# Weight differences by adding transfers on GpSimd's queue, with the first weights stored with the opposite sign

## The chip, the cores and the metric

The kernel runs on one core of a Trainium2 chip. The metric is the device time of one execution in microseconds (us). Smaller is better. Engine names are those of the profile: PE is TensorE's matmul, PEld its weight load, DVE is VectorE, ACT is ScalarE, POOL is GpSimd, SP is SyncE, which issues the transfers (DMAs).

## The reference: what is computed

A gated recurrence per batch and head gives y, and y, laid out as 3072 tokens by 384 features, goes through a maxout layer:

```python
mag = np.sqrt(a_re * a_re + a_im * a_im)
scale = np.minimum(mag, 0.999) / (mag + 1e-06)
a_re_n, a_im_n = (a_re * scale, a_im * scale)
for t in range(S):                      # S = 768, state S is 48 x 48, complex
    ...
    S_re, S_im = (new_re + kv, new_im)  # new = a * S, kv = k (outer) v
    y[:, :, t] = np.einsum('bhd,bhde->bhe', q[:, :, t], S_re)

h = np.maximum(np.maximum(x @ w1, x @ w2), x @ w3)   # x: 3072 x 384, w: 384 x 768
return (h @ w_out).astype(np.float32)                # w_out: 768 x 384
```

There are 4 batches and 8 heads of 48. The four weights arrive as 64-bit floats and have to be made 32-bit ones. The other inputs are 32-bit.

## The kernel before

**Tiling.** A step g takes 128 tokens of two batches (C = 2, called x and y), and there are 12 steps. Per step, the gates are turned into sums of logarithms and angles (ACT and DVE), queries and keys are scaled, transposed on PE and multiplied, and the state is carried from step to step. The result y, features by tokens, goes through the maxout layer.

**The maxout layer by differences.** max(w1 x, w2 x, w3 x) is w1 x + max(0, (w2 - w1) x, (w3 - w1) x). So ws[1] and ws[2] hold differences, `larger` (line 824) makes max(0, .) on ACT and the second max on DVE, and the part of w1 goes past the maximum as one 384 by 384 matrix wp = w1 times w_out. `product` (line 424) makes wp on PE: T transposes ws[0] block by block, t copies that to `third`, M multiplies by wo into the tiles wm, and m copies wm to wp on ACT. In step 0, `up_one` (line 811) makes the layer for x and y apart, with matmul groups named U, then index f of the 256 columns, then the weight, then x or y: U22y is block 8 times the tokens of y. From step 1 on, `up` takes both together.

**The weights.** `weight_blocks` (line 373) cuts them into 12 blocks of 128 partitions by 768: 0, 3, 6 are w1, 1, 4, 7 are w2, 2, 5, 8 are w3, and 9 to 11 are w_out. The name of a step is W, a letter, and the block. WL loads the 64-bit words with SP. Then, with low and high the halves of each word: a takes the absolute value of high (ACT), b clamps it (DVE), c shifts it left by 3 bits (DVE), d turns low into 2 + low / 2^51 in the block's final place (ACT), e adds the bits of that to the shifted part as integers (DVE), f joins high's sign to the result and writes the block (DVE). For blocks 1, 2, 4, 5, 7, 8 a last step g subtracts w1's block in place, on DVE (line 422).

**What sets the order.** SCHEDULE (line 21) is a text with every step of the program. `program` (line 964) emits them in that order, and `Bound` (line 191) ties each instruction of an engine behind the one emitted before it on the same engine, so each engine runs its own in the order of the text. An instruction waits for its operands, whoever makes them. What concerns POOL: `constants_early` (line 278) runs ahead of the text; then the text has, of POOL's steps, CL (`constants_late`, line 309), Z3, Z4 and Z2 in this order. CL makes the masks maskd and masko, with KB as scratch, and zeroes the two tiles atm. Z3, Z4 and Z2 zero buffers that `third` has used: vbs[3], us["k"][2], vbs[2]. In the text, Wg2 and Wg4 stand at line 32, CL at line 33, the three Z at line 34, Wg5 at line 36, Wg1 at 37, Wg7 at 41 and Wg8 at 42.

The first reader of CL's results is g0x at line 33, a DVE instruction (COPY_PREDICATED atm<-maskd,A) that `scores` (line 688) emits. Behind it on DVE come, among others, mulai and stt (gates of step 1) and uqy, the queries of y that PE then transposes (tpqy). PE's order there is M0, M1, tpqy, M2, tpky.

The profile gives line 200 for nearly every instruction, since `Bound` issues them; they are told apart by tile and operation.

Of the kernel before, what the change touches and what calls it, by code (L numbers as in the profile page):

```python
# [15 lines left out]
AF = mybir.ActivationFunctionType  # L16
OP = mybir.AluOpType
# [119 lines left out]
def kernel(  # L137
# [18 lines left out]
    DM = H * D  # L156
# [31 lines left out]
    T = {}  # L188
# [18 lines left out]
    pe, dve, act, pool, sp = (Bound(e) for e in (nc.tensor, nc.vector, nc.scalar, nc.gpsimd, nc.sync))  # L207
    mm = pe.matmul

    def banks(nm, n=None):  # L210

        ps = psum.tile([P, 2, 512], FP, tag="ps", name=nm)
        T["ps"] = ps
        return ps if n is None else ps.rearrange("p a n -> p (a n)")[:, 0:n]
# [4 lines left out]
    def activation(func, **kw):  # L219

        need = SETS.get(func, T.get("set"))
        if need != T.get("set"):
            act.preload_act_table_set(need)
            T["set"] = need
        act.activation(func=func, **kw)

    def once(key, make):

        if key not in T:
            T[key] = make()  # L230
        return T[key]
# [137 lines left out]
    wp, wo = wx[:, 0:KD], wx[:, KD:]  # L369
# [3 lines left out]
    def weight_blocks():  # L373

        blocks, n = [], FF // 3
        for f in range(3):
            for w, src in zip(ws, (moe_w1, moe_w2, moe_w3)):
                cols = slice(f * n, (f + 1) * n)
                blocks.append((w[:, :, cols], src.rearrange("(i p) m -> p i m", p=P)[:, :, cols]))
        for f in range(0, KF, 2):  # L380
            blocks.append((wo[:, f:f + 2], moe_w_out.rearrange("(i p) m -> p i m", p=P)[:, f:f + 2]))
        return blocks
# [16 lines left out]
    def weight_step(i, step):  # L399

        dst, src = blocks[i]
        n, m = dst.shape[1:]
        raw = T["raw", i].rearrange("p n (m w) -> p n m w", w=2)
        low, high = raw[:, :, :, 0].bitcast(U32), raw[:, :, :, 1]
        ex = xhx[:, 0:KD] if i in EX else xhx[:, KD + KF:]
        ex = ex.rearrange("p f t -> p (f t)").rearrange("p (n m) -> p n m", n=n).bitcast(I32)
        if step == "a":
            activation(out=ex.bitcast(FP), in_=high.bitcast(FP), func=AF.Abs)
        elif step == "b":
            dve.tensor_scalar(out=ex.bitcast(FP), in0=ex.bitcast(FP), scalar1=2.0 ** -15, scalar2=LAST,  # L410
                              op0=OP.max, op1=OP.min)
        elif step == "c":
            dve.tensor_single_scalar(out=ex, in_=ex, scalar=3, op=OP.logical_shift_left)
        elif step == "d":
            activation(out=dst, in_=low, func=AF.Copy, scale=2.0 ** -51, bias=2.0)
        elif step == "e":
            dve.tensor_tensor(out=ex, in0=ex, in1=dst.bitcast(I32), op=OP.add)
        elif step == "f":
            dve.scalar_tensor_tensor(out=dst.bitcast(I32), in0=high, scalar=-0x80000000, in1=ex,
                                     op0=OP.bitwise_and, op1=OP.bitwise_or)  # L420
        else:
            dve.tensor_tensor(out=dst, in0=dst, in1=blocks[i - i % 3][0], op=OP.subtract)

    def product(name, f):

        third = (vbs[2].rearrange("p c i d -> p (c i d)"), vbs[3].rearrange("p c i d -> p (c i d)"),
                 us["k"][2].rearrange("p h d -> p (h d)"))[f][:, 0:2 * DM]
        if name == "T":
            ps = T["wt", f] = banks("wt", 2 * DM)
            for u in range(2):  # L430
                for d in range(KD):
                    o = u * DM + d * P
                    pe.transpose(out=ps[:, o:o + P], in_=ws[0][:, d, (2 * f + u) * P:(2 * f + u + 1) * P], identity=ident)
        elif name == "t":
            act.copy(out=third, in_=T["wt", f])
        elif name == "M":
            for d in range(KD):
                ps = once(("wm", d // 2), lambda: banks("wm"))[:, d % 2, 0:DM]
                for u in range(2):
                    mm(out=ps, lhsT=third[:, u * DM + d * P:u * DM + (d + 1) * P], rhs=wo[:, 2 * f + u],  # L440
                       start=2 * f + u == 0, stop=2 * f + u == KF - 1)
        elif f < 2:
            n = 2 - f
            act.copy(out=wp[:, 2 * f:2 * f + n], in_=T["wm", f][:, 0:n, 0:DM])

    def flat(t):
        return t.rearrange("p c h d -> p (c h d)")
# [473 lines left out]
    def run(name, g):  # L921
# [12 lines left out]
        elif name[0] in "TtMm" and name[1:].isdigit():  # L934
            product(name[0], int(name[1:]))
        elif name[0] == "W":
            i = int(name[2:])
            weight_load(i) if name[1] == "L" else weight_step(i, name[1])
        elif name[0] in "Uu" and name[1:].isdigit():
            up(g, int(name[1]), int(name[2]), name[0])  # L940
        elif name[0] in "Uu" and name[1:3].isdigit():
            up_one(2 * g + "xy".index(name[3]), int(name[1]), int(name[2]), name[0])
        elif name in SEVEN or name in ("ox", "oy") and g > 0:
            seven(g, name)
        elif name[0] == "J":
            join(name[1])
        elif name[-1] in "01" and gates(g, [int(name[-1])], name[:-1]):
            pass
        elif gates(g, list(range(C)), name):
            pass  # L950
        else:
            c = "xy".index(name[-1])
            x, name = g * C + c, name[:-1]
            if name in ("Lr", "Li"):
                load_a(g, c, *(("ar", a_re) if name == "Lr" else ("ai", a_im)))
            elif name in ("Lk", "Lq"):
                load_kq(g, c, *(("k", k) if name == "Lk" else ("q", q)))
            elif name == "Lv":
                load_v(g, c)
            else:  # L960
                assert angles(g, c, name) or turns(g, c, name) or factors(x, name) or scores(x, name) \
                    or state(x, name) or outputs(x, name) or project(x, name), name
# [6 lines left out]
    blocks = weight_blocks()  # L969
# [38 lines left out]
```

## Time and profile before

| what | us |
|---|---|
| median of 3 runs | 585.9 (585.05 to 587.58) |
| span of the profiled execution | 585.0 |
| busy PE | 537.6 (92%) |
| busy PEld | 454.6 (78%) |
| busy DVE | 506.0 (86%) |
| busy ACT | 439.4 (75%) |
| busy POOL | 15.5 (3%) |

The span runs from the first instruction to the last of the profiled execution; the three timed runs took 585.05 to 587.58 us in all. In a timeline, the first column is the start in us from the span's start, the second the duration (of all the instructions, where several in a row are merged and counted with x), then engine, line, operation, output <- inputs, shape, and in brackets how long the engine was idle just before and what it waited for. A tile's name is without its number: w can be any of ws or the gates' tile w. "SPq" is SP's queue of transfers. PEclk is the clock that TensorE was granted, 1.00 for full speed.

### The profile page before, as it was taken

How to read it: one execution, taken by the hardware profiler on the slowest of the kernel's cores; microseconds unless marked ns; L12 is line 12 of the kernel's file. 1: busy time of each engine (PE TensorE's matmuls, PEld its weight loads, DVE VectorE, ACT ScalarE, POOL GpSimd, SP SyncE). 2: the span in 40 equal slices, each digit the busy share in tenths (PEclk: the TensorE clock that was granted, in tenths of full speed). 3: DMA queues.
4: the chain of work that ended last, by engine and by line, in shares of the span. 5: the costliest groups of instructions: out<-in, count | busy, mean ns of one | idle time of the engine just before them, and what ended most of it. 6: DMA issues, size and time to landing. Idle time of an engine off the chain costs nothing.

```text
span 585.0 us, 22777 instructions
## 1 busy us (share of the span) xinstructions
PE 537.6 (92%) x10118; PEld 454.6 (78%) x10118; DVE 506.0 (86%) x784; ACT 439.4 (75%) x740; POOL 15.5 (3%) x50
## 2 busy tenths in 40 slices
PE   2649979898999999999999999999999999999897
PEld 0336668767888888888898888898887888888886
DVE  5999999979898999999889889989998999877504
ACT  7999999857788778788788987887896797643110
POOL 8100100000000000000000000000000000000000
PEclk9778999989999999999999999999999999999999
DMA  8984134414204214223223233143043031010000
GB/s 269 251 181 109 56 85 76 90 33 80 43 18 107 46 35 93 43 48 80 43 53 76 41 62 75 33 97 60 14 97 70 7 73 37 3 43 2 30 0 27
DMA packets 136544, 39.24 MB, mean 67 GB/s; under 512 B 129152, under 2 KB 132224, under 8 KB 136448
## 3 DMA queue, kind: packets, MB, share of 16 engines
q1 hardware_dynamic: 136448, 37.80, 29.2%
q8 instruction: 79, 1.29, 0.9%
q14 instruction: 17, 0.14, 0.1%
HBM read 33.03 MB, written 4.72 MB: 65 GB/s over the span
## 4 chain that ended last, share of the span: by engine, by line
PE 82%; ACT 11%; issue 3%; DMA 1%; DVE 1%; SPq 1%; DVEq 0%; ACTq 0%
PE up L200 31%; PE op L200 22%; PE y L200 6%; PE A L200 5%; PE tp L200 4%; PE dk L200 4%; PE sums L200 3%; PE cs L200 2%; PE wm L200 2%; ACT xhx L200 2%; PE B L200 1%; PE F L200 1%; ACT w L200 1%; ACT e L200 1%; ACT L200 1%
## 5 line engine op out<-in xcount | busy, mean ns | idle before, releaser
L200 PE MATMUL up<-xhx,w 128*128 128x256 f32 x792 | 176.5, 382 | 0.9 <-ACT xhx L200 0.6
L200 PEld LDWEIGHTS up<-xhx,w 128*128 128x128 f32 x792 | 148.7, 190 | 21.6 <-ACT xhx L200 1.1
L200 DVE TENSOR_TENSOR Q<-Q,f 112x512 f32<-112x512 f32 (+2 forms) x72 | 68.3, 952 | 9.4 <-ACT Q L200 9.4
L200 ACT ACT_TABLE_LOAD x48 | 61.6, 1283 | 1.6 <-PEq L992 0.8
L200 PE MATMUL op<-wo,xhx 128*128 128x192 f32 (+1 forms) x220 | 47.4, 363 | 0.0
L200 DVE TENSOR_TENSOR xhx<-xhx,up 128x768 f32<-128x768 f32 x22 | 20.9, 952 | 26.8 <-PE up L200 26.8
L200 PEld LDWEIGHTS op<-wo,xhx 128*128 128x128 f32 x220 | 37.0, 190 | 6.6 <-issue 0.3
L200 PE MATMUL y<-atm,vb 128*32 128x64 f32 x1152 | 39.0, 221 | 2.1 <-issue 2.1
L200 ACT ACTIVATE f<-F 48x280 f32<-48x280 f32 x96 | 38.4, 400 | 3.5 <-DVE g L200 2.3
L200 DVE TENSOR_TENSOR ot<-ot,op 128x192 f32<-128x192 f32 (+1 forms) x66 | 26.7, 418 | 15.7 <-ACT ot L200 12.0
L200 PE MATMUL y<-QG,g 112*32 112x64 f32 x1408 | 38.4, 219 | 0.0
L200 ACT COPY atm<-B 32x128 f32<-32x128 f32 x96 | 24.6, 256 | 18.2 <-DVE atm L200 12.9
L200 PE MATMUL A<-Q,K 112*32 112x80 f32 x1536 | 33.2, 234 | 5.5 <-issue 5.5
L200 ACT COPY ot<-op 128x192 f32<-128x192 f32 (+1 forms) x13 | 4.5, 344 | 44.2 <-PE op L200 44.2
L200 PEld LDWEIGHTS y<-atm,vb 128*32 128x32 f32 x1152 | 32.4, 109 | 6.4 <-issue 3.4
L200 PEld LDWEIGHTS A<-Q,K 112*32 112x32 f32 x1536 | 28.0, 110 | 10.4 <-issue 9.1
L200 PEld LDWEIGHTS y<-QG,g 112*32 112x32 f32 x1408 | 34.9, 109 | 1.3 <-issue 1.2
L200 PE MATMUL op<-wo,strassen 128*128 128x192 f32 x176 | 33.5, 332 | 0.3 <-issue 0.3
L200 DVE COPY_PREDICATED atm<-masko,A 128x256 f32<-128x256 uint8 x72 | 31.1, 432 | 1.1
L200 ACT COPY Q<-tp 112x1024 f32<-112x1024 f32 x24 | 24.4, 1019 | 8.7 <-PE tp L200 8.7
L200 PEld LDWEIGHTS op<-wo,strassen 128*128 128x128 f32 x176 | 28.6, 190 | 3.0 <-issue 2.1
L200 PE MATMUL op<-w,strassen 128*128 128x192 f32 x176 | 30.7, 327 | 0.0
(145 smaller groups left out, 1144.0 us busy)
## 6 DMA issues: line engine op xcount, KB each, us to landing
ar<-in_a_re_dram SPq DMA_DIRECT2D x24, 192.0 KB
ai<-in_a_im_dram SPq DMA_DIRECT2D x24, 192.0 KB
q<-in_q_dram SPq DMA_DIRECT2D x96, 48.0 KB
vb<-in_v_dram SPq DMA_DIRECT2D x96, 48.0 KB
k<-in_k_dram SPq DMA_DIRECT2D x96, 48.0 KB
out_dram<-ot SPq DMA_DIRECT2D x24, 192.0 KB
w<-in_moe_w_dram SPq DMA_DIRECT2D x3, 768.0 KB
xhx<-in_moe_w_dram SPq DMA_DIRECT2D x3, 768.0 KB
```

Source lines behind the costliest of these rows:

```text
L200: ins = f(*a, **kw)
```

## The change

The w1 blocks (0, 3, 6) are made with the opposite sign: step d gives -(2 + low / 2^51), so the sign bit is set, and step f flips it by high's sign with an exclusive or. The difference w2 - w1 is then a sum, w2 + (-w1), and step g is a transfer from SBUF to SBUF that adds its source to its destination, issued on GpSimd's queue in place of DVE's subtraction. Since wp is made from w1, the copies of wm to wp turn the sign back. SCHEDULE is as it was.

```diff
         elif step == "d":
-            activation(out=dst, in_=low, func=AF.Copy, scale=2.0 ** -51, bias=2.0)
+            sign = -1.0 if i in (0, 3, 6) else 1.0
+            activation(out=dst, in_=low, func=AF.Copy, scale=sign * 2.0 ** -51, bias=sign * 2.0)
         elif step == "e":
             dve.tensor_tensor(out=ex, in0=ex, in1=dst.bitcast(I32), op=OP.add)
         elif step == "f":
             dve.scalar_tensor_tensor(out=dst.bitcast(I32), in0=high, scalar=-0x80000000, in1=ex,
-                                     op0=OP.bitwise_and, op1=OP.bitwise_or)
+                                     op0=OP.bitwise_and, op1=OP.bitwise_xor)
         else:
-            dve.tensor_tensor(out=dst, in0=dst, in1=blocks[i - i % 3][0], op=OP.subtract)
+            pool.dma_start(out=dst, in_=blocks[i - i % 3][0], accum_op=OP.add)
...
             n = 2 - f
-            act.copy(out=wp[:, 2 * f:2 * f + n], in_=T["wm", f][:, 0:n, 0:DM])
+            activation(out=wp[:, 2 * f:2 * f + n], in_=T["wm", f][:, 0:n, 0:DM], func=AF.Copy, scale=-1.0)
```

The source and the destination of one transfer are 128 partitions of three runs of 256 floats, 384 KB.

## The prediction

> **What bounds the kernel now.** I read the page's 40 slices first, then busy times by stretch, then the chain of work that ended last, then the timelines of the engines that the change touches.
>
> ```profile
> PE   2649979898999999999999999999999999999897
> DVE  5999999979898999999889889989998999877504
> ACT  7999999857788778788788987887896797643110
> ```
>
> One digit is 14.6 us. PE is full from slice 7 (102 us) to the end, and the whole chain is 82% PE, so what happens earlier counts by how late it makes PE. The edited steps end before 99 us, where DVE and ACT are both at 9. The stretch from 52 to 101 us (length, then busy PE, PEld, DVE, ACT, POOL, then clock, DMA share, GB/s) says the same: ACT is idle for only 1.7 us of 49, DVE for 2.8.
>
> ```profile
> 52.00:101.00 49.00, 44.24 (x837) 35.19 (x826) 46.21 (x71) 47.26 (x80) 1.64 (x3) 1.00 0.37 87
> ```
>
> The chain there is PE from 48 to 66.6 us, ACT to 87.9, then PE.
>
> ```profile
> 52.93 7.94 PE wm L200 x24
> 60.87 0.59 PE tp L200 x16
> 61.46 4.07 PE wm L200 x12
> ...
> 66.59 0.87 ACT K L200
> ```
>
> **What is removed.** Six subtractions leave DVE (Wg2, Wg4 at 52.05 us, Wg5 73.18, Wg1 77.39, Wg7 91.94, Wg8 97.89). They start 0.87 us apart from the next instruction, so DVE gets back 6 x 0.87 = 5.2 us. I count it at nothing, apart from one term below: after the first two DVE waits anyway (mulw at 54.49 stands until ACT's L, which does not move), and around the other four the chain runs through ACT. If ACT did not cover it, 5.2 us would be the most that could be won.
>
> The edits of sign cost nothing: bitwise_xor takes bitwise_or's place in the same two-input instruction (0.95 us), the activation of step d has other constants, and the two copies of wm to wp (128x384 in 0.48 us, 128x768 in 0.80) become activations, whose rows of these sizes read 0.49 to 0.51 and 0.81 to 0.85. At worst 0.06 us each on ACT.
>
> **What is moved: the constants on POOL.** This is the step that decides. POOL takes its instructions in order:
>
> ```profile
> 8.40 0.41 POOL L200 MEMSET KB<- 128x384 f32 x1
> ...
> 15.53 1.28 POOL L200 MEMSET atm<- 128x512 f32 x2
> 60.99 0.75 POOL L200 MEMSET vb<- 128x768 f32 x1 [44.18 <-PE wm L200]
> 65.59 0.21 POOL L200 MEMSET uk<- 128x128 f32 x1 [3.85 <-PE wm L200]
> 65.73 0.74 POOL L200 MEMSET vb<- 128x768 f32 x1
> ```
>
> The last line is Z2. Its buffer was last read by the first 12 of the 24 wm matmuls, so it was free at about 57 us; it ran at 65.73, behind Z4, which waited. A waiting instruction holds what follows. In SCHEDULE, Wg2 and Wg4 stand ahead of CL (the masks and the zeroed atm). Today CL has nothing ahead of it and runs at 8.40. After the change it stands behind two transfers, whose operands are finished by these:
>
> ```profile
> 50.32 0.95 DVE L200 SCALAR_TENSOR_TENSOR w<-xhx 128x768 int32<-128x768 int32 x1
> 51.19 0.95 DVE L200 SCALAR_TENSOR_TENSOR w<-strassen,xhx 128x768 int32<-128x768 int32 x1
> ...
> 55.83 0.72 DVE L200 COPY_PREDICATED atm<-maskd,A 128x512 f32<-128x512 uint8 x1
> ```
>
> The third line is g0x, the first reader of CL. From CL's start to the end of the first atm memset is 15.53 + 0.64 - 8.40 = 7.8 us. Let D be the time that POOL spends on issuing one transfer. Then CL starts at 51.27 + 2D (not before 52.14 + D), and g0x is late by 51.27 + 2D + 7.8 - 55.83 = 3.2 + 2D.
>
> No POOL transfer is in this trace. The nearest rows are SP's issues: a weight load, also 384 rows, takes 0.37 us at its shortest; the longest took 5.28 us, behind nine others. So D lies between 0.37 and 2.64 (two in a row taking what that one took). SP's short rows are nearest in form, but part 3 calls their queue hardware_dynamic, GpSimd's would not be that, and a transfer that adds reads two operands. I take the geometric middle of 0.37 and 5.28, 1.4 us. **g0x is late by 6.0 us** (4.5 to 8.5).
>
> DVE is in order, so everything behind g0x is as late: mulai and stt, for which ACT's L (59.57) and atan (60.30) wait; and uqy (59.44), for which PE's transposition at 60.80 waits, 0.4 us behind it. ACT and PE have no idle time to take this up. Below I give times in the old frame, with this delay left out.
>
> **PE's clock.** PE now stands idle for about 5.5 us at 60.9. Today's trace has a 1.67 us gap at 115.45, with this behind it (same columns):
>
> ```profile
> 118.00:122.00 4.00, 4.00 (x9) 2.16 (x8) 3.96 (x8) 2.38 (x4) 0.00 (x0) 0.61 0.01 4
> ```
>
> The granted clock fell to 0.61 for 4 us: 4 x 0.39 = **1.6 us** lost. I add it once, on the 12 wm matmuls, which ACT's K waits for. It could be 0: gaps of 1.2 us cost nothing.
>
> **The four later transfers.** Each has an issue D and a landing T on the path that the subtraction's 0.95 us had. T: the first load of 192 KB was used 2.9 us after its issue began, the first of 768 KB 6.3 us after, so 384 KB lies at 4.0 by size, less SP's 0.44 of issuing: T = 3.5 (2.5 to 6.3). D + T = 4.9.
> - Wg1 and Wg5 stand behind Wf5 (ends 72.79): 72.79 + 2.8 + 3.5 = 79.1. U01x starts at 79.61, U12x at 81.67. In time by 0.5.
> - Wg7: Wf7 ends 89.76, lands 94.7. U21y starts at about 93.7, the third of three groups of 12 from 90.84. Late by 1.0.
> - Wg8: Wf8 ends 97.64, here 0.87 earlier as Wg7 no longer stands ahead of it on DVE: 96.77 + 4.9 = 101.7. U22y:
>
> ```profile
> 99.34 1.60 PE L200 MATMUL up<-xT,w 128*128 128x128 f32 x12
> ```
>
> Late by **2.3 us**, Wg7's 1.0 within it (0 to 6). From here PE is full, so it stays. By the Trainium skill (DMA: Bandwidth & Descriptors, "Anatomy of one DMA — SWDGE (gpsimd) path") such a transfer costs about 2.0 us fixed plus its bytes at 436 GB/s, 2.9 us for 384 KB; with that for D + T, Wg8 would be late by 0.3 and the sum 2 us lower. No run here shows one yet.
>
> **Sum.** 6.0 + 1.6 + 2.3 = 9.9 us on a span of 585.0. The profiled execution's span lies 0.9 us under the median, 585.9; I take that as the time around it and predict 585.9 + 9.9 = 595.8.
>
> **Rivals.**
> - *Cheap transfers* (D = 0.37, D + T = 2.9, clock not lost): 4.5 + 0.3 = 4.8, so 590.7. For it: SP's short rows. Against: SP's queue is not GpSimd's. 0.18.
> - *Dear transfers* (D = 2.64, T = 6.3): g0x 8.5, Wg8 96.77 + 8.94 - 99.34 = 6.4, clock 1.6: 16.5, so 602.4; if issuing is slower still, above that. The DMA share is 0.86 from 52 to 56 us, so there is traffic to share with. 0.13.
> - *Faster*: POOL does not stand at a transfer's wait but hands it to a queue, so CL is done by 55.83 as today, and DVE's 5.2 us is what bounds the stretch from 73 to 98. It decides from the point where ACT and PE wait for DVE there rather than DVE for them. At most 585.9 - 5.2 = 580.7. Against: the order Z4, Z2 above, and ACT idle for only 1.7 us. 0.04.
> - *No difference*: CL is in time as in that case and ACT covers DVE, with at most ACT's idle 1.7 us won: 584.2 to 586. 0.07.
>
> **Chances.** Forecast (592 to 600) 0.58, and the rivals as given. The range 589 to 603 takes in the bounds of D and T and leaves out the last two rivals and about half of the dear one. A measurement here tells about 0.5%, 2.9 us, from no change: faster 0.04, same 0.07, slower 0.89.
>
> **What would show it.** In the profile after: POOL's memset of KB at 53 to 55 us instead of 8.40, and the atm memsets at 60 to 63; DVE's idle time before COPY_PREDICATED atm<-maskd put down to POOL, some 5 to 7 us; PE's transposition tp<-uq 6 us later, and the granted clock lower behind that gap; PE waiting for a transfer before the up group of 12 that is now at 99.34. If KB's memset is still at 8.40, the main step is wrong, and the time is that of the last two rivals. If g0x is late but K's copy is not, ACT had slack that I did not see.

## The result and the profile after

The changed kernel takes 602.3 us (median of 3 runs, 600.5 to 602.8) against 585.9. The ratio is 1.026 (95% interval 1.022 to 1.030). Its profiled execution spans 601.1 us, 16.1 more than before. By the medians it is slower by 16.4 us, by the ratio by 15.2 (13.1 to 17.3); 9.9 were forecast.

| group of matmuls on PE | before | after | late by |
|---|---|---|---|
| tpky, behind the wm matmuls | 65.46 | 71.81 | 6.4 |
| U11x | 75.96 | 82.02 | 6.1 |
| U01x | 79.61 | 91.18 | 11.6 |
| U12x and U02x | 81.67 | 94.50 | 12.8 |
| U11y | 87.90 | 99.77 | 11.9 |
| U02y | 95.65 | 108.61 | 13.0 |
| U22y | 99.34 | 114.14 | 14.8 |
| op<-wo,hT | 102.72 | 119.16 | 16.4 |
| end of the span | 585.0 | 601.1 | 16.1 |

The 16.4 us that `op<-wo,hT` is late arise between 51 and 119 us, in three places. What follows is not a mere shift. At 115 us the profile of the kernel before has a gap of 1.67 us on PE with a slow stretch behind it, the one from which the prediction took the price of the clock. The changed kernel has 1.21 us there and full speed behind it, so 2.2 us are made up. These are the rows behind the gap, first before, then after:

```profile
117.52 3.90 PE L200 MATMUL op<-wo,xT 128*128 128x384 f32 x6
```
```profile
133.46 2.20 PE L200 MATMUL op<-wo,xT 128*128 128x384 f32 x6
```

The next group is 14.2 us late. The other 1.9 us of the span come in small steps, up and down, after the last of the adding transfers. I did not trace them.

In POOL's timeline of the changed kernel (start, duration, operation), CL now stands behind two transfers:

```profile
51.16 2.71 POOL L200 DMA_DIRECT2D w<-w  x2 [43.07 <-DVE w L200]
52.87 1.44 POOL L200 MEMSET KB<- 128x384 f32 x1
...
58.84 0.99 POOL L200 MEMSET atm<- 128x512 f32 x2
...
79.17 2.58 POOL L200 DMA_DIRECT2D w<-w  x2 [6.35 <-DVE w L200]
101.44 1.27 POOL L200 DMA_DIRECT2D w<-w  x1 [19.68 <-DVE w L200]
109.08 1.28 POOL L200 DMA_DIRECT2D w<-w  x1 [6.37 <-DVE w L200]
```

DVE's timeline shows g0x waiting for that:

```profile
59.40 0.73 DVE L200 COPY_PREDICATED atm<-maskd,A 128x512 f32<-128x512 uint8 x1 [4.19 <-POOL atm L200]
```

PE's timeline shows what became of it, and the waits for the later transfers, in brackets (before, U01x started without a wait, which is the first row here):

```profile
79.61 1.60 PE L200 MATMUL up<-xT,w 128*128 128x128 f32 x12
```

```profile
64.11 1.10 PE L200 MATMUL tp<-ident,uq 64*112 64x64 f32 x16 [3.37 <-DVE uq L200]
65.15 6.73 PE L200 MATMUL wm<-wo,uk 128*128 128x384 f32 x12
...
91.18 2.90 PE L200 MATMUL up<-xT,w 128*128 128x128 f32 x12 [5.46 <-DMA w<-w]
...
106.52 1.57 PE L200 MATMUL up<-xT,w 128*128 128x128 f32 x12 [0.87 <-DMA w<-w]
...
114.14 2.31 PE L200 MATMUL up<-xT,w 128*128 128x128 f32 x12 [1.98 <-DMA w<-w]
116.25 3.07 PE L200 MATMUL op<-wo,xT 128*128 128x384 f32 x6
```

The four lines with a wait are the story. Two things beside the waits matter: the 12 wm matmuls take 6.73 us where they took 4.14, and U01x's group takes 2.90 where 1.60 is usual. Both run behind a gap, at a lower clock (0.50 from 91 to 94 us, for U01x). The stretch from 64 to 72 us (columns as in the prediction; the third number from the end is the clock) shows it:

```profile
64.00:72.00 8.00, 7.89 (x34) 4.56 (x36) 7.17 (x10) 4.73 (x5) 0.06 (x1) 0.60 0.00 0
```

From 52 to 101 us ACT was idle for 1.7 us before. Now PE, DVE and ACT all stand:

```profile
52.00:101.00 49.00, 36.89 (x671) 27.62 (x660) 32.74 (x50) 36.27 (x61) 11.29 (x23) 0.86 0.46 99
```

### The profile page after: what moved, and what is told of

Its sections match the earlier page's. It is cut to its first block, busy times and chain, and to the rows that moved or that the text cites. A ratio compares the mean times of both kernels' runs of the same rounds, so it can differ in the third digit from the quotient of the medians.

```text
span 601.1 us, 22789 instructions
## 1 busy us (share of the span) xinstructions
PE 542.1 (90%) x10118; PEld 458.3 (76%) x10118; DVE 501.2 (83%) x778; ACT 439.9 (73%) x740; POOL 20.5 (3%) x56
## 4 chain that ended last, share of the span: by engine, by line
PE 79%; ACT 8%; issue 5%; DMA 3%; DVE 2%; POOL 2%; SPq 0%; DVEq 0%; POOLq 0%
PE up L200 31%; PE op L200 22%; PE y L200 6%; PE A L200 4%; PE tp L200 4%; PE dk L200 4%; DMA w<-w 3%; PE sums L200 3%; PE cs L200 2%; PE F L200 1%; PE B L200 1%; ACT xhx L200 1%; ACT w L200 1%; ACT e L200 1%; PE wm L200 1%
## 5 line engine op out<-in xcount | busy, mean ns | idle before, releaser
L200 DVE TENSOR_TENSOR Q<-Q,f 112x512 f32<-112x512 f32 (+2 forms) x72 | 68.2, 951 | 12.0 <-ACT Q L200 11.9
```

Source lines behind the costliest of these rows:

```text
L200: ins = f(*a, **kw)
```

## The experiments

The theory at this point: three prices, the order on POOL (6 us), Wg1's late landing behind Wg5's transfer and a load of SP (6 us), and Wg7 and Wg8 (4 us). The rivals: the signs cost something, or transfers of this kind slow the kernel by their traffic wherever they stand. Ratios are to the kernel before on the same chip, with 95% intervals; one per cent is 5.9 us.

### The order on POOL

CL is moved ahead of the two transfers, in SCHEDULE:

```diff
-f2y:0 f0y:0 Wf2:0 Wf4:0 Wg2:0 Wg4:0 f1y:0 pw:1 lnw:1 expL:1 mulw:1 Lqy:0 Lky:0 mky:0 afy:0 sign:1 say:0 Lix:2
-WL5:0 Lqx:1 Cdx:0 Ax:0 CL:0 g0x:0 M0:0 M1:0 Lry:2 Wa5:0 sby:0 mulai:1 mqy:0 stt:1 g1x:0 Wb5:0 uqy:0 tpqy:0 Wd5:0
+f2y:0 f0y:0 Wf2:0 Wf4:0 CL:0 Wg2:0 Wg4:0 f1y:0 pw:1 lnw:1 expL:1 mulw:1 Lqy:0 Lky:0 mky:0 afy:0 sign:1 say:0 Lix:2
+WL5:0 Lqx:1 Cdx:0 Ax:0 g0x:0 M0:0 M1:0 Lry:2 Wa5:0 sby:0 mulai:1 mqy:0 stt:1 g1x:0 Wb5:0 uqy:0 tpqy:0 Wd5:0
```

> CL (masks, zeroed atm) is put ahead of Wg2 and Wg4 in SCHEDULE; all six adding transfers stay. Theory A (order on POOL costs 6 us): KB's memset is back at about 8.4 us, DVE does not wait 4.2 us at g0x, PE's clock stays at full through the 12 wm matmuls (4.1 us instead of 6.7), and the time falls from 602.3 by about 6 to 596. The later waits for transfers (5.5, 0.9, 2.0 us) stay. Rival B (the six transfers slow the engines wherever they stand, and the wait at g0x is only where that shows): the 12 wm matmuls or the transposition ahead of them stay late and the time stays within 2 us of 602.

Measured: 595.5 us, ratio 1.019 (1.016 to 1.023), which is 6.8 us under the changed kernel's median and 3.8 under it by the ratios. PE's timeline is that of before up to there:

```profile
60.74 0.66 PE L200 MATMUL tp<-ident,uq 64*112 64x64 f32 x16
61.33 4.14 PE L200 MATMUL wm<-wo,uk 128*128 128x384 f32 x12
```

The clock is back as well. The later waits stay (5.6 and 2.2 us). Not all of the 6 us comes back: U11x is at 77.21, 1.25 later than before, since ACT now waits for a load:

```profile
ACT e L200 <- DMA ar<-in_a_re_dram: 1.8, 1, 1.8
```

In the changed kernel the wait at g0x had hidden this one. It comes up again below.

The same price from the other side: no transfer adds, but CL is held on POOL.

```diff
-            pool.dma_start(out=dst, in_=blocks[i - i % 3][0], accum_op=OP.add)
+            dve.tensor_tensor(out=dst, in0=dst, in1=blocks[i - i % 3][0], op=OP.add)
...
         if name == "CL":
+            pool.tensor_copy(out=biases[:, 3:4], in_=ws[1][:, 0, FF // 3:FF // 3 + 1])
             constants_late()
```

> No adding transfer at all (signs as in the changed kernel, step g on DVE), but CL is held on POOL behind Wg4 by a copy of one column of that block, as two transfers hold it in the changed kernel. It measures the order on POOL by itself. Theory A: KB's memset at about 54 us, DVE waits 3.5 to 5 us at g0x, PE's transposition is as late, and the time is 3.5 to 7 above the kernel before, the upper part if PE's clock falls behind the gap. Rival B (the wait at g0x is hidden, and the transfers' traffic alone makes the changed kernel slower in that stretch): within 1.5 us of the kernel before.

Measured: 591.0 us, ratio 1.009 (1.006 to 1.013), that is 5.4 us (3.5 to 7.5). g0x waits 3.71 us and the 12 wm matmuls take 6.23 us:

```profile
53.30 0.18 POOL L200 COPY biases<-w 128x1 f32<-128x1 f32 x1 [45.11 <-DVE w L200]
```
```profile
58.98 0.73 DVE L200 COPY_PREDICATED atm<-maskd,A 128x512 f32<-128x512 uint8 x1 [3.71 <-POOL atm L200]
```
```profile
63.69 1.10 PE L200 MATMUL tp<-ident,uq 64*112 64x64 f32 x16 [3.62 <-DVE uq L200]
64.72 6.23 PE L200 MATMUL wm<-wo,uk 128*128 128x384 f32 x12
```

(POOL, DVE and PE of this kernel.) One copy of a single column that waits costs 5.4 us, with no traffic of transfers: the order is enough.

### The signs alone

> The signs as in the changed kernel, but step g is a DVE addition again, so no transfer adds. Theory A (signs cost nothing): 585.9 within 1.5 us. Rival B (the exclusive or, the activation in place of the copy or the stored sign costs time): above 589.

The edit keeps the changed signs of steps d and f and of the copies to wp, and makes step g an addition on DVE. Measured: 585.3 us, ratio 1.002 (1.000 to 1.003). The signs cost at most 2 us, and nothing that can be told from no change.

### Wg1's late landing

The load of block 8's raw words is left out (`if i != 8:` ahead of `sp.dma_start` in `weight_load`); the block is made of what lies in its room.

> The changed kernel without the 768 KB load of block 8 of the weights (its steps run on what lies in the room), which starts 0.2 us ahead of Wg5's and Wg1's transfers. It leaves that block's weights out. Theory A (Wg1 lands late since its transfer shares the 16 DMA engines with that load): the wait of 5.5 us ahead of U01x shrinks to 0 to 1.5 us and the time falls to 595 to 598. Rival B (an adding transfer is slow by itself when two stand in a row): the wait stays at 4.5 us or more and the time within 2 us of 602.

Measured: 598.1 us, ratio 1.024 (1.020 to 1.027). The wait ahead of U01x is 2.34 us, between the two forecasts:

```profile
87.98 2.90 PE L200 MATMUL up<-xT,w 128*128 128x128 f32 x12 [2.34 <-ACT L L200]
```

It is put down to ACT's L, which had nothing to do with this group; the operands of U01x are xT and w. The trace has Wg1's transfer land at 87.85, 0.13 us ahead of the group, so the wait is for the transfer. The load accounts for 3.1 of the 5.5 us, and theory A is half right.

The packets show how. In the changed kernel, from 79.2 to 83.8 us, SP's queue has 941 packets (0.89 MB) and GpSimd's has none, though both transfers have been issued by 81.8. Without the load, 394 of the 800 packets of the two transfers lie in that stretch.

Next, Wg5 goes back to DVE, so that Wg1's transfer stands alone:

```diff
+            if i in (1, 2, 4, 7, 8):
                 pool.dma_start(out=dst, in_=blocks[i - i % 3][0], accum_op=OP.add)
+            else:
+                dve.tensor_tensor(out=dst, in0=dst, in1=blocks[i - i % 3][0], op=OP.add)
```

> The changed kernel with Wg5 alone back on DVE as an addition; Wg1's transfer now stands alone behind Z2 on POOL, and its operands are ready long before, so it is issued at about 73 us instead of 80. CL still stands behind Wg2 and Wg4. Theory A (two transfers in a row behind Wf5 and the load beside them make Wg1 late): no wait ahead of U01x, the waits ahead of U21y and U22y (0.9 and 2.0 us) as before, time 602.3 less 5 to 7, so 595 to 597. Rival B (a transfer that adds lands late wherever it is): the wait at U01x stays above 3 us and the time within 2.5 us of 602.

Measured: 593.9 us, ratio 1.015 (1.010 to 1.019), 8.4 us under the changed kernel's median and 6.7 by the ratios. Wg1 is issued at 72.56, U01x starts with no wait, and the other two stay:

```profile
85.45 1.69 PE L200 MATMUL up<-xT,w 128*128 128x128 f32 x12
```
```profile
PE up L200 <- DMA w<-w: 3.3, 2, 2.0
```

So Wg1 was late for three reasons at once. It stood behind Wg5 in POOL's order, though its own operands had been ready for nearly 40 us. Its transfer ran behind Wg5's: the second of the two landed 8.0 us after its issue began even without the load, where a single one takes 4.9 (72.56 to 77.49 here). And both ran against the load that the same Wf5 releases: in the version with four transfers, further down, Wg5's stands alone beside that load and takes 9.1 us (75.86 to 84.98).

### Is it the adding?

> The changed kernel with the six transfers copying -w1 instead of adding it, so the differences are left out. Theory A (the time from issue to landing is mostly the sharing of the queues and the fixed part of a transfer, not the addition): the issue on POOL stays at 1.3 us each, the wait ahead of U22y stays at 1.5 to 2.3 us and the one ahead of U01x above 4; 600 to 603. Rival B (the addition, with its second operand to be read, is what is slow): U22y's wait falls below 0.8, U01x's below 3, and the time to 597 or less.

The edit takes `, accum_op=OP.add` away. Measured: 593.7 us, ratio 1.013 (1.009 to 1.017). Theory A falls on the issue, on both waits and on the time. POOL's timeline, and the part on DMA queues (packets, MB, share of 16 engines), first of the changed kernel, then of this one:

```profile
q0 software_dynamic: 2400, 2.36, 2.5%
```
```profile
q0 software_dynamic: 672, 2.36, 1.2%
```
```profile
51.41 1.64 POOL L200 DMA_DIRECT2D w<-w  x2 [43.07 <-DVE w L200]
...
102.73 0.76 POOL L200 DMA_DIRECT2D w<-w  x1 [6.90 <-DVE w L200]
```

For the same bytes an adding transfer is 400 packets instead of 112, takes 0.025 x 601.1 / 6 = 2.5 us of all 16 DMA engines instead of 0.012 x 590.4 / 6 = 1.2, and 1.27 us of POOL instead of 0.76. The wait at U22y is 1.35 us instead of 1.98, there is none at U21y, and 3.53 instead of 5.46 at U01x. Rival B has the time right, but its thresholds for the waits are not met: a plain copy would have been late too. Part of the 8.6 us between the two medians is the clock: here PE stood 3.08 us ahead of the transposition and the 12 wm matmuls took 4.14 us, at full speed, so 2.6 us of the gain come by way of the clock and not from earlier landings.

### What DVE's relief is worth

> Step g is left out altogether, so neither DVE nor POOL takes differences; the rest is the changed kernel. It is the most that taking the six subtractions off DVE can bring. Theory A (ACT and PE cover them): 583 to 586, at most 1.7 us under the kernel before. Rival B (DVE bounds 73 to 98 us): 579.5 to 582.

Step g is replaced by `pass`. Measured: 586.0 us, ratio 1.000 (0.998 to 1.002). The six subtractions, 5.2 us of DVE, are worth nothing that can be told here (at most 1.2 us), so in this order of the program no way of moving them off DVE could have won.

### What is left, and the best version

CL first and Wg1 behind Wf1, all six as transfers:

```diff
-t2:0 Wf1:0 Qcx:0 Q2x:0 expe:1 expw:1 lne:1 Wd2:0 Wc2:0 QBx:0 Q1x:0 nfy:0 T1:0 tpkx:0 Enx:0 kEnx:0 relu:1 Lnop:1
+t2:0 Wf1:0 Wg1:0 Qcx:0 Q2x:0 expe:1 expw:1 lne:1 Wd2:0 Wc2:0 QBx:0 Q1x:0 nfy:0 T1:0 tpkx:0 Enx:0 kEnx:0 relu:1 Lnop:1
```

> CL ahead of Wg2 and Wg4, and Wg1's transfer issued right behind Wf1, some 35 us earlier; all six transfers stay. Theory A: neither g0x nor U01x waits; what is left is Wg7 and Wg8 with about 1 and 2 us and the clock behind that, so 588 to 591. Rival B (transfers of this kind slow the kernel by their traffic, not by when they land): 594 or more.

Measured: 589.5 us, ratio 1.008 (1.005 to 1.011), 4.4 us. PE waits 1.35 and 1.98 us for Wg7 and Wg8, as expected. Then these two go back to DVE, and CL goes to the front (ahead of WL2):

> CL ahead of all transfers, Wg1 right behind Wf1, Wg2, Wg4 and Wg5 as transfers, Wg7 and Wg8 as additions on DVE (they have no time to land). Theory A: no wait for a transfer is left, and DVE's four subtractions bring nothing: within 1.5 us of the kernel before. Rival B (four instructions less on DVE do help): 1.5 to 3.5 us under it.

Measured: 589.3 us, ratio 1.006 (1.003 to 1.008): 3.3 us slower, a miss. No PE group has its start put down to an adding transfer, but ACT waits for SP's load of ar. The chain of this kernel, then the stretch from 50 to 60 us of this kernel and of the kernel before (second number from the end: share of the DMA engines):

```profile
57.16 5.67 DMA ar<-in_a_re_dram
62.83 0.02 issue
62.85 0.84 ACT e L200
```
```profile
50.00:60.00 10.00, 10.00 (x92) 5.96 (x90) 7.66 (x12) 9.86 (x17) 2.54 (x2) 1.00 0.89 181
```
```profile
50.00:60.00 10.00, 10.00 (x92) 6.09 (x91) 9.38 (x14) 9.85 (x16) 0.00 (x0) 1.00 0.50 123
```

The transfers of Wg2 and Wg4 start at 51.24, beside SP's loads of block 5 of the weights and of q. The ar load is issued at 57.16 instead of 55.84 and lands at 62.83; ACT waits 2.27 us where it had no wait before. In the version with all six as transfers the same two start at 54.22, 3 us later, ar is issued at 55.33, and ACT does not wait for it, which points to the collision and not to the traffic as such. To test that, Wg2 and Wg4 go back to DVE as well, so only Wg1 and Wg5 are transfers:

> As the version with four transfers, but Wg2 and Wg4 are additions on DVE too, so only Wg1 (right behind Wf1) and Wg5 are transfers. Theory A (in the version with four, the transfers of Wg2 and Wg4 delay SP's load of ar, for which ACT waited 2.3 us; DVE's relief brings nothing): ACT does not wait for that load, and the time is within 1.5 us of the kernel before. Rival B (any transfer on GpSimd's queue costs, wherever it stands): 2 us or more above it.

Measured: 586.1 us, ratio 1.001 (0.999 to 1.003): no difference from the kernel before. ACT does not wait for ar at 60 us. U01x stops for 1.45 us within the group, as it does for 0.96 in the version with four, while Wg5's transfer runs; the profile names no cause, and PE's slack behind it takes it up. A transfer with time to land and a quiet queue costs nothing that can be told, and wins nothing. No version beat the kernel before.

## Why the prediction was right or wrong

The direction was right, and so was the step called decisive, the order on POOL. The range held too, but only by 0.7 us at its upper end, and with some 6 us for Wg1 in the time, which the sum had put at nothing; that is luck. The likeliest value was 6.5 us short, for the most part by one term.

- **DVE's relief: nothing.** Right; without step g the ratio is 1.000.
- **The signs: nothing.** Right.
- **The order on POOL: 6.0 us at g0x and 1.6 us of clock, 7.6.** Measured 6.1 to 6.4 us in the changed kernel, 5.4 alone. Its parts were off in opposite ways. The issue time D was 1.27 to 1.36 us for 1.4. CL took 5.5 us from its start to the first atm memset (53.88 in the chain to 59.37) instead of 7.8. So g0x waited 4.2 us and came at 59.40, 3.6 us later than before instead of 6.0, and PE's transposition 3.3 later; of the signs that were named, the wait of 5 to 7 us and the transposition 6 us later did not come. The clock cost more: 2.6 us on the wm matmuls and 0.4 on the transposition.
- **"Wg1 and Wg5 ... In time by 0.5": this step failed.** U01x waited 5.46 us and ran at half speed, and about 5.8 of it remained at U11y. T was taken between two loads that had been measured with other traffic, and the two transfers were taken to land 3.5 us behind their issue each. In fact both and the 768 KB load started within 2 us and landed 11.9 us after Wg5's issue began. The step ignored that Wf5, which releases Wg5, also frees the room for that load, so SP issues it at 78.97, 0.2 us ahead, and that two transfers in a row land one behind the other. The load's part is 3.1 us of the wait; putting Wg5 back removes all of it.
- **Wg7 and Wg8: 2.3 us.** Their waits were 0.87 and 1.98, 2.9 in all, plus about 1.6 us of clock behind the second, which was put at nothing. D + T was 4.9 us (109.08 to 114.0), as worked out. That is partly luck: the 4.9 came from loads, which do not add, and a plain copy takes 3.4 (102.73 to 106.1). The Trainium skill's fit (DMA: Bandwidth & Descriptors, "Anatomy of one DMA — SWDGE (gpsimd) path") gave an estimate of 2.9 us; the trace shows 4.9 for an adding transfer and 3.4 for the plain copy, so the measurement decides.
- **The rivals.** The dear one gave 602.4, and the measured time is 602.3, but not for its reason: it had 8.5 us at g0x and 6.4 at Wg8, and nothing at Wg1. *Faster* and *no difference* needed POOL to go on past a waiting transfer; it does not: KB's memset went from 8.40 to 53.88, and a single waiting copy does the same.

The parts fit the whole, no closer than they are known. By the ratios they are 5.4 us (CL held alone, 3.5 to 7.5), 6.7 (Wg1, good to about 3.6 either way) and 4.4 (what is left without these two, 2.7 to 6.1). They make 16.5, against 15.2 for the whole by the ratio and 16.4 by the medians. That they meet the latter so closely is chance. Not tried was how much of CL's longer or shorter time DVE causes.

## What to carry to other kernels

Before work moves to a queue that looks idle, list what follows on that queue in program order: the first instruction that waits holds all of it, and constants that once ran at the start run when the wait ends. A transfer that takes the place of an instruction needs its whole time to landing between producer and reader, counted with every transfer that the same event releases, and two in a row count twice. If leaving the moved work out altogether changes nothing, as here, moving it can't win while the order stays as it is.

## What the runs showed of the hardware

- A transfer of 384 KB in SBUF that adds takes about twice the DMA engines' time of a copy (2.5 against 1.2 us of all 16) and 400 packets against 112; POOL is busy with its issue for 1.27 us against 0.76. Alone it lands 4.9 us after its issue begins, beside a load of 768 KB issued 0.2 us earlier 9.1 us; a plain copy alone lands after 3.4.
- PE's granted clock fell behind some gaps and not behind others, and their length alone does not decide it. Behind gaps of 3.37, 3.46, 3.62 and 3.86 us ahead of the wm matmuls, the 8 us from 64 to 72 read 0.60 to 0.69, and these matmuls took 6.22 to 6.73 us; behind one of 3.08 they took 4.14. A wait of 1.98 us ahead of U22y was followed by a group of 2.31 us in the changed kernel and of 1.58 in two versions. And in the kernel without step g a gap of 0.74 us, behind others of that stretch, was followed by 3 us at half speed:

```profile
87.40:90.40 3.00, 3.00 (x14) 2.78 (x16) 2.71 (x5) 2.97 (x4) 0.00 (x0) 0.50 0.24 44
```

- POOL's constants took longer beside a busy DVE. The same instructions took 8.4 us from 8.40 in the kernel before, 6.0 us while DVE mostly waited for them, and 12.6 us from 41.65 in the version with Wg1 early, where six selections alone read

```profile
46.39 6.20 POOL L200 TENSOR_SCALAR_AFFINE_SELECT KB<-KB 128x64 f32<-128x64 f32 x6
```

against 1.72 in the changed kernel. No run isolates what in DVE's work slows them.
